# TensorE's loop from eight to nine rounds, two ring slots for the last V blocks, w_up in two parts and a one-matmul residual, in a decode kernel that streams a KV cache

## The chip, the cores and the metric

The kernel runs on one core of a Trainium2 chip. The metric is the device time of one execution in microseconds (us), the median of several executions. A profile is one further execution with the hardware profiler on; its span is 1.6 to 1.8 us shorter than the device time of that execution in the two main profiles. TensorE is the matrix engine, VectorE the vector engine, ScalarE the activation engine; GpSimd and SyncE are the other two. In the profile they are PE (PEld is its loading of weights), DVE, ACT, POOL and SP. SyncE issues nearly all transfers, on one queue (11560 of the 11568 packets in the page of the kernel before) that sixteen DMA engines serve together: the trace has sixteen reports for each transfer, and a transfer has landed with the last of them. The granted clock is the share of TensorE's full clock that the profile shows for a stretch of time. A run over 1.5% above the fastest of its kernel would count as slow.

## The reference, cut to what matters

```python
B, Sq, D = 1, 1, 512;  Hq, Hkv, Sk, Dh = 32, 8, 65536, 128;  F = 1792      # bfloat16
h  = x + A(layernorm(x))       # q = x@wq; softmax(q k^T / sqrt(Dh)) v; @wo
h2 = h + B(layernorm(h))       # (sigmoid(x@w_gate) * (x@w_up)) @ w_down
```

One token attends to a cache of 65536 positions and 8 KV heads. K and V are 134 MB each; with the weights 282.3 MB have to come from memory, each byte once.

## The kernel before: the parts that matter

K and V come in 32 blocks of 4 MB each (8 heads, 4 blocks per head). Of a K block, VectorE transposes eight pieces and TensorE multiplies them with the head's query; the softmax of a head follows after its fourth block; V products (`PV`) run one head behind. A ring of four 4 MB slots holds what has landed. The order of the loads, and who frees a slot:

```python
order = [("wq", 0)]
order += [("K", b) for b in range(NR)]
for b in range(NR, NB):
    order += [("K", b), ("V", b - NR)]
order += [("V", NB - 4), ("V", NB - 3), ("V", NB - 2), ("V", NB - 1), ("wg", 0), ("wu", 0), ("wd", 0)]
for i, ld in enumerate(order):
    slot_of[ld] = i % NSLOT
    prev[ld] = order[i - NSLOT] if i >= NSLOT else None
# a load waits for freed(prev): K by VectorE's transposes ("F"), V by its product ("PV")
# wo (4 MB, three transfers) is issued between V28 and V29
```

So a steady state has K in slots 1 and 3 and V in 0 and 2, but the last loads go round all four.

TensorE and VectorE run their instructions in a hardware loop. For TensorE a round `i` holds, for `r` in 0 to 3, part `A{r}` (scores of K block `4i+r`) and part `B{r}` (product of V block `4(i-1)+r`); the B parts are skipped in round 0:

```python
P.rounds = {"pe": (0, HKV), "dve": (1, HKV)}
...
with eng.Fori(lo, hi) as i:
    for p in order:
        with ExitStack() as cond:
            if lo not in parts[e][p]:
                cond.enter_context(eng.If_ne(i.val[eng.engine], lo))
            for o, w in zip(parts[e][p][hi - 1], plan[p]):
                put(e, eng, o, w)
```

What follows the eight rounds (the four V products of the last head, the wo product, the second block) is straight-line code. Its end, cut:

```python
# w_gate (gu0), the residual, then w_up (gu1)
for i, (nm, bank) in enumerate((("wg", GB), ("wu", UB))):
    for kt in range(4):
        for c in range(4):
            op("pe", ... matmul(ps(bank, ...), lhsT=hc[:, kt:kt + 1], rhs=wv[:, kt, c * FG:(c + 1) * FG]), ["hc", nm] ...)
    if i == 0:                      # residual h, 16 fp32 matmuls of 1x32 (32 passes)
        for g in range(4):
            for kt in range(4):
                op("pe", ... matmul(dst, lhsT=hT[1][:, kt:kt + 1], rhs=identf[:, 32 * g:32 * g + 32], start=(kt == 0) ...))
# sg = tanh (ScalarE), hh = product, hhT = transpose (VectorE)
for i, (r0, r1) in enumerate(WD_SPLIT):       # [(0, 7), (7, 12), (12, 14)]: w_down lands in three parts
    for r in range(r0, r1):
        for g in range(4):
            op("pe", ... matmul(ps(YB, 0, 128, ...), lhsT=hhT[:, 32 * r:32 * r + 1], rhs=wd_v[:, r, g * 128:(g + 1) * 128]), ["hhT", f"wd{i}"] ...)
# cast to bfloat16 (VectorE), output transfer
```

## Time and profile before

| quantity | value |
|---|---|
| device time | 664.56 us median of 3 runs (664.40 to 664.81) |
| profiled span | 662.6 us |
| TensorE / VectorE busy | 64% / 53% |
| bytes read | 282.33 MB, 426 GB/s over the span |
| last V block's first part released | 643.98 us |
| last matmul / output transfer issued | 659.93 / 660.30 us |

The first view is the page: busy time of the engines with its share of the span and the number of instructions, the DMA engines' busy share in 40 slices of 16.6 us (tenths, 9 means 90% or more), the bytes per second in each slice, and the queues with the share of the sixteen DMA engines' time. This is the kernel before.

```profile
PE 424.0 (64%) x2385; PEld 80.5 (12%) x1617; DVE 350.6 (53%) x443; ACT 38.1 (6%) x106; POOL 5.4 (1%) x12
DMA  9999999999999999999999999999999999999997
GB/s 380 439 420 435 437 423 437 433 423 441 429 425 441 425 431 439 423 436 433 425 437 433 425 439 431 425 437 431 427 439 425 433 435 425 437 433 410 426 427 292
q1 hardware_dynamic: 11560, 282.33, 99.3%
q8 instruction: 4, 0.07, 0.0%
q14 instruction: 2, 0.02, 0.0%
```

No slice but the last is below 90%, and the data queue's packets occupy 99.3% of all DMA engines' time. No compute engine is near that. Queues 8 and 14 carry a few packets of instructions.

The second view is the chain of waits, in order of time (start, us, what): from the middle of the span.

```profile
169.13 29.65 DMA ring<-in_A_k_cache_dram
198.81 9.13 DVE ktw L439 x8
207.98 29.65 DMA ring<-in_A_k_cache_dram
```

A K block is issued at 169.13, lands 29.65 us later, is transposed in 9.13 us, which frees its slot for the issue at 207.98. The period is 38.85 us, in which two K and two V blocks pass: 16.78 MB / 38.85 us = 432 GB/s. The 29.65 us from issue to landing are mostly time behind other blocks in the queue: at 432 GB/s the 4.19 MB of one block take 9.7 us (estimate).

The third view is the timeline of the end (start, us, engine, line, operation, in square brackets the idle time before and what ended it). `PS<-ring,PT_sb` are V products, `PS<-ring,hc` w_gate and w_up, `PS<-ring,hhT` w_down.

```profile
626.94 3.21 PE L529 MATMUL PS<-ring,PT_sb 128*16 128x512 bf16 x32 [3.32 <-DMA ring<-in_A_v_cache_dram]
...
643.98 3.22 PE L529 MATMUL PS<-ring,PT_sb 128*16 128x512 bf16 x32 [1.79 <-DMA ring<-in_A_v_cache_dram]
650.31 0.16 DVE L624 SCALAR_TENSOR_TENSOR hc<-PS,hT 128x4 bf16<-128x4 f32 x1 [0.50 <-PE PS L358]
652.27 1.20 PE L640 MATMUL PS<-identf,hT 128*1 128x32 f32 x32
655.17 0.93 PE L632 MATMUL PS<-ring,hc 128*1 128x448 bf16 x16 [1.70 <-DMA ring<-in_B_w_up_dram]
657.80 0.91 PE L656 MATMUL PS<-ring,hhT 128*1 128x128 bf16 x28 [1.70 <-DVE hhT L651]
658.91 1.02 PE L656 MATMUL PS<-ring,hhT 128*1 128x128 bf16 x28 [0.20 <-DMA ring<-in_B_w_down_dram]
659.98 0.29 DVE L660 CAST y_sb<-PS 128x128 bf16<-128x128 f32 x1 [2.24 <-PE PS L656]
```

The V products shown (V29, V31; V30 at 636.65 is left out), w_up's matmuls and the second part of w_down each start when their bytes land. The residual's 32 passes (652.27) run while TensorE waits for w_up.

### The profile page before, as it was taken

To read this page: it belongs to the slowest core of one execution; us is meant where nothing else is said; L and a number is where in the kernel's file an instruction comes from. 1 tells how busy PE (TensorE), PEld (TensorE's weight loads), DVE (VectorE), ACT (ScalarE), POOL (GpSimd) and SP (SyncE) were. 2 spreads that over 40 slices of the span, in tenths; PEclk is the share of its full clock that TensorE was granted. 3 is DMA by queue.
4 is the path that set the end of the run, shared out by engine and by line. 5 is a ranking of instruction groups with operands and counts; after the bars stand their busy time and mean duration, and the time that the engine had idled before them with its cause. 6 is when DMAs were issued, how large, how long until landed. Compare 5 with 4: busy or idle time off the path is not lost.

```text
span 662.6 us, 4910 instructions
## 1 busy us (share of the span) xinstructions
PE 424.0 (64%) x2385; PEld 80.5 (12%) x1617; DVE 350.6 (53%) x443; ACT 38.1 (6%) x106; POOL 5.4 (1%) x12
## 2 busy tenths in 40 slices
PE   2787487548676575576665576765856667556744
PEld 1100010011010110011100111001100111001222
DVE  3598855556337654347555463466643565553002
ACT  0200200020000200020000200002000200002000
POOL 2000000000000000000000000000000000000000
PEclk9799687678877677776866688766878867766877
DMA  9999999999999999999999999999999999999997
GB/s 380 439 420 435 437 423 437 433 423 441 429 425 441 425 431 439 423 436 433 425 437 433 425 439 431 425 437 431 427 439 425 433 435 425 437 433 410 426 427 292
DMA packets 11568, 282.42 MB, mean 426 GB/s; under 512 B 1193, under 2 KB 2218, under 8 KB 2602
## 3 DMA queue, kind: packets, MB, share of 16 engines
q1 hardware_dynamic: 11560, 282.33, 99.3%
q8 instruction: 4, 0.07, 0.0%
q14 instruction: 2, 0.02, 0.0%
q10 hardware_dynamic: 2, 0.00, 0.0%
HBM read 282.33 MB, written 0.00 MB: 426 GB/s over the span
## 4 chain that ended last, share of the span: by engine, by line
DMA 71%; DVE 22%; PE 6%; issue 1%; SPq 0%; ACT 0%
DMA ring<-in_A_k_cache_dram 62%; DVE ktw L439 20%; DMA ring<-in_A_v_cache_dram 4%; DMA ring<-in_B_w_down_dram 3%; PE PS L452 2%; DMA ring<-in_A_wq_dram 2%; PE PS L394 1%; PE PS L529 1%; DVE M_sb L444 1%; PE PS L451 1%; SPq L313 0%; DVE PT_sb L501 0%; PE PS L656 0%; PE PS L478 0%; PE PS L485 0%
## 5 line engine op out<-in xcount | busy, mean ns | idle before, releaser
L439 DVE STREAM_TRANSPOSE ktw<-ring 128x1024 f32<-128x1024 f32 x256 | 291.8, 1207 | 166.3 <-DMA ring<-in_A_k_cache_dram 165.3
L452 PE MATMUL PS<-ktw 128*128 128x512 bf16 x768 | 271.4, 452 | 54.2 <-DVE ktw L439 54.2
L451 PE MATMUL PS<-ktw 128*128 128x512 bf16 x256 | 119.0, 465 | 116.7 <-DVE ktw L439 114.9
L529 PE MATMUL PS<-ring,PT_sb 128*16 128x512 bf16 x1024 | 75.1, 444 | 12.8 <-DMA ring<-in_A_v_cache_dram 11.6
L451 PEld LDWEIGHTS PS<-ktw 128*128 128x128 bf16 x256 | 27.7, 108 | 432.8 <-issue 274.4
L501 DVE STREAM_TRANSPOSE PT_sb<-P_sb 128x512 bf16<-128x512 bf16 x32 | 20.2, 684 | 37.4 <-PE PS L539 36.0
L529 PEld LDWEIGHTS PS<-ring,PT_sb 128*16 128x16 bf16 x1024 | 30.6, 116 | 56.5 <-issue 30.0
L444 DVE TENSOR_REDUCE M_sb<-PS 128x1 f32<-128x512 f32 x32 | 19.9, 684 | 25.6 <-PE PS L451 25.6
L487 ACT ACTIVATE negmax<-PS 128x1 f32<-128x1 f32 x8 | 1.4, 171 | 545.8 <-PE PS L485 545.8
L491 ACT ACTIVATE P_sb<-PS,negmax 128x512 bf16<-128x512 f32 x32 | 21.5, 685 | 0.3
L508 DVE TENSOR_REDUCE lsum<-PS 128x1 f32<-128x4 f32 x8 | 1.3, 162 | 29.8 <-PE PS L506 29.8
L394 PE MATMUL PS<-ring,xz 128*8 128x512 bf16 x32 | 9.7, 478 | 7.4 <-DMA ring<-in_A_wq_dram 7.4
L354 DVE COPY hT<-PS 128x4 f32<-128x4 f32 x2 | 1.3, 629 | 24.9 <-PE PS L566 24.9
L478 PE MATMUL PS<-identf,gm 128*1 128x128 f32 x16 | 3.3, 292 | 17.0 <-DVE gm L476 17.0
L536 ACT ACTIVATE po_sb<-PS,rl 128x512 bf16<-128x512 f32 x8 | 5.7, 708 | 39.7 <-PE PS L529 39.7
L539 PE MATMUL PS<-sel_bf,po_sb 128*128 128x4 bf16 x32 | 2.1, 169 | 8.0 <-ACT po_sb L536 8.0
L485 PE MATMUL PS<-one_f,gmrep 1*128 1x1 f32 x16 | 4.0, 317 | 5.0 <-DVE gmrep L482 5.0
L491 ACT ACTIVATION_READ_ACCUMULATOR P_sb<-PS,negmax 128x1 f32 x32 | 6.5, 203 | 0.0
L369 POOL TENSOR_TENSOR rstd<-ve,nhalf 128x1 f32<-128x1 f32 x2 | 1.1, 553 | 645.7 <-DVE ve L367 645.7
L577 PE MATMUL PS<-ktw,O 128*1 128x512 bf16 x28 | 6.2, 379 | 0.0
L394 PEld LDWEIGHTS PS<-ring,xz 128*8 128x8 bf16 x32 | 3.2, 102 | 13.5 <-issue 11.3
L480 DVE TENSOR_REDUCE gmj<-PS 1x4 f32<-1x128 f32 x8 | 2.2, 278 | 4.1 <-PE PS L478 4.1
(85 smaller groups left out, 68.8 us busy)
## 6 DMA issues: line engine op xcount, KB each, us to landing
ring<-in_A_k_cache_dram SPq DMA_DIRECT2D x32, 4096.0 KB, 29.6
ring<-in_A_v_cache_dram SPq DMA_DIRECT2D x31, 4096.0 KB, 30.4
ring<-in_A_wq_dram SPq DMA_DIRECT2D x1, 4096.0 KB, 12.3
ring<-in_A_v_cache_dram SPq DMA_DIRECT2D x1, 3072.0 KB, 32.3
ktw<-in_A_wo_dram SPq DMA_DIRECT2D x1, 2048.0 KB, 9.6
ktw<-in_A_wo_dram SPq DMA_DIRECT2D x2, 1024.0 KB, 13.0
ring<-in_B_w_gate_dram SPq DMA_DIRECT2D x1, 1792.0 KB, 35.1
ring<-in_B_w_up_dram SPq DMA_DIRECT2D x1, 1792.0 KB, 24.9
```

Source lines behind the costliest of these rows:

```text
L394: op("pe", lambda e, kt=kt, n=n, last=last: e.matmul(ps(1, 0, 512, 0, 8), lhsT=xz[:, kt * 15 + 7 - n: kt * 15 + 15 - n], rhs=wq_v[:, kt, n ...
L439: op("dve", lambda e, d=dst, sr=src: e.transpose(d, sr), deps, f"T{b}.{c}", to="T")
L444: op("dve", lambda e, u=u: e.tensor_reduce(M_sb[:, u % 4:u % 4 + 1], ps(u % NS, 0, 512), AX.X, ALU.max), [f"S{b}.{NC - NR + k}"], f"mx{u}" ...
L451: return e.matmul(out, lhsT=lhsT, rhs=rhs, start=start, stop=stop)
L452: return e.add_instruction(mybir.InstMatmult(name=nc.get_next_instruction_name(), engine=mybir.EngineType.PE, ins=[e.lower_ap(rhs), e.lowe ...
L478: op("pe", lambda e: e.matmul(ps(MISC, 0, 128, 0, 1), lhsT=gm[:, :], rhs=identf[:, :], start=True, stop=True), [f"gm{h}"], f"gmT{h}", to="Q")
L485: op("pe", lambda e: e.matmul(ps(MISC, 128, 129), lhsT=gmrep[0:1, :], rhs=one_f[0:1, 0:1], start=True, stop=True), [f"gmrep{h}"], f"neg{h}")
L491: op("act", lambda e, b=b: e.activation(P_sb[:, (b % 4) * 512:(b % 4 + 1) * 512], ps(b % NS, 0, 512), AF.Exp, bias=negmax[:, k:k + 1], sca ...
L501: op("dve", lambda e, b=b: e.transpose(PT_sb[:, (b % 4) * 512:(b % 4 + 1) * 512], P_sb[:, (b % 4) * 512:(b % 4 + 1) * 512]), [f"E{b}", f"o ...
L529: op("pe", lambda e, lhsT=lhsT, tq=tq, t0=t0, c=c: e.matmul(ps(PO, 0, 512, 32 * tq, 32 * tq + 16), lhsT=lhsT, rhs=ring[:, s * SLOT + t0 * ...
L536: op("act", lambda e: e.activation(po_sb[:, :], ps(PO, 0, 512), AF.Copy, scale=rl[:, :]), [f"PV{NR * h + NR - 1}", f"rl{h}"], f"po{h}", to ...
L577: op("pe", lambda e, r=r, src=src, n=n, end=end: e.matmul(ps(YB, 0, D, 0, 1), lhsT=src[:, r:r + 1], rhs=ktw[:, r * D:(r + 1) * D], start=( ...
```

## The change

The intent: let the last head's four V products run in a ninth round of the same loop, instead of being written out again, so that TensorE's program gets shorter. The loop needs the same slot and the same waits for a V block in every round, so the last V blocks stay in slots 0 and 2. The K slots 1 and 3 are then free early and take w_gate, w_up and w_down. At the end, w_up is loaded in two parts so that three quarters of its product can run before the rest lands, and the residual becomes one fp32 matmul with a prepared operand `hz`. The diff, cut to its core (cuts marked with `...`):

```diff
-            order = [p for p, r in seq if r == hi - 1]
+            order = self.order[e]
...
-                        if lo not in parts[e][p]:
-                            cond.enter_context(eng.If_ne(i.val[eng.engine], lo))
-                        for o, w in zip(parts[e][p][hi - 1], plan[p]):
+                        if runs == [hi - 1]:
+                            cond.enter_context(eng.If_eq(reg, hi - 1))
+                        else:
+                            if runs[0] != lo:
+                                cond.enter_context(eng.If_ne(reg, lo))
+                            if runs[-1] != hi - 1:
+                                cond.enter_context(eng.If_lt(reg, runs[-1] + 1))
+                        for o, w in zip(parts[e][p][runs[-1]], plan[p]):
...
-            slot_of[ld] = i % NSLOT
-            prev[ld] = order[i - NSLOT] if i >= NSLOT else None
+            if ld[0] == "V" and ld[1] >= NB - NR:
+                slot_of[ld] = slot_of["V", ld[1] - 2]
+                prev[ld] = ("V", ld[1] - 2)
+            elif ld[0][0] == "w" and i:
+                slot_of[ld] = 3 if ld[0] == "wd" else 1
+                prev[ld] = ("K", NB - 1 if ld[0] == "wd" else NB - 2)
+            else: ...                                   # as before
...
+        W_SPLIT = {"wg": [(0, 4)], "wu": [(0, 3), (3, 4)]}
+        W_AT = {"wg": 0, "wu": 4 * FF}
...
-        P.rounds = {"pe": (0, HKV), "dve": (1, HKV)}
+        P.rounds = {"pe": (0, HKV + 1), "dve": (1, HKV)}
+        P.order = {"pe": ["A0", "B0", "L", "A1", "B1", "A2", "B2", "A3", "X", "C", "B3"], ...}
...                        # X: wait for the fourth V block, i = 1 to 7; C: only in the ninth round (i = 8)
...                        # L: wo product of heads 0-27, only in the ninth round
-            op("dve", lambda e: e.tensor_copy(yr[:, :], ps(YB, 0, D, 0, 1)), ["yr"], "yrs")
+            op("dve", lambda e: e.tensor_tensor(yr[:, :], ps(YB, 0, D, 0, 1), x_row[:, :], ALU.add), ["yr"], "yrs")
...
-                for g in range(4):
-                    for kt in range(4):
-                        ...                             # the residual's 16 fp32 matmuls
+                op("pe", lambda e: e.matmul(ps(YB, 0, 128), lhsT=gsel[:, :], rhs=hz[:, :], start=True, stop=False, ...), ["hz"])
```

Besides, one zeroing matmul and one matmul that added `x` are dropped; VectorE gets three small operations.

More of the change, by code (lines that the diff above doesn't have):

```diff
@@ L44, in __init__ @@
         self.rounds = {}
+        self.order = {}
         self.part = {}
@@ L147, in run @@
                 s2 = {}
-                w = [waits_of(e, o, s2, off, True) for o in parts[e][p][r]]
+                w = [waits_of(e, o, s2, off, len(parts[e][p]) > 1) for o in parts[e][p][r]]
                 assert plan.setdefault(p, w) == w, (p, r)
@@ L155, in run @@
                         off[k] = off.get(k, 0) + n
-            regs = {}
             with eng.Fori(lo, hi) as i:
                 for p in order:
+                    runs = sorted(parts[e][p])
+                    reg = i.val[eng.engine]
                     with ExitStack() as cond:
-                        if lo not in parts[e][p]:
-                            cond.enter_context(eng.If_ne(i.val[eng.engine], lo))
-                        for o, w in zip(parts[e][p][hi - 1], plan[p]):
+                        if runs == [hi - 1]:
+                            cond.enter_context(eng.If_eq(reg, hi - 1))
+                        else:
+                            assert runs == list(range(runs[0], runs[-1] + 1)) and runs[0] - lo < 2
+                            if runs[0] != lo:
[3 more added lines that the diff above has]
+                        for o, w in zip(parts[e][p][runs[-1]], plan[p]):
                             put(e, eng, o, w)
@@ L204, in bass_sequential_preLN__gqa_block_cached__glu_gated_glu__decode_kernel @@
         yr = sb("yr", [1, 512], fp32)
+        gsel = sb("gsel", [128, 128], fp32)
+        hz = sb("hz", [128, 128], fp32)
         scr = sb("scr", [1, 64], fp32)
@@ L275, in bass_sequential_preLN__gqa_block_cached__glu_gated_glu__decode_kernel @@
         for i, ld in enumerate(order):
-            slot_of[ld] = i % NSLOT
-            prev[ld] = order[i - NSLOT] if i >= NSLOT else None
+            if ld[0] == "V" and ld[1] >= NB - NR:
[4 more added lines that the diff above has]
+                prev[ld] = ("K", NB - 1 if ld[0] == "wd" else NB - 2)
+            else:
+                slot_of[ld] = i % NSLOT
+                prev[ld] = order[i - NSLOT] if i >= NSLOT else None
         def freed(ld):
@@ L296, in bass_sequential_preLN__gqa_block_cached__glu_gated_glu__decode_kernel @@
                 w = B_w_gate if k == "wg" else B_w_up
-                dma("sp", lambda e, d=dst, w=w: e.dma_start(d[:, 0:4 * FF].rearrange("p (k n) -> p k n", k=4),
-                    w.rearrange("(p k) n -> p k n", p=128)), f"r{s}", deps, k)
+                dst, src = dst[:, W_AT[k]:W_AT[k] + 4 * FF], w.rearrange("(p k) n -> p (k n)", p=128)
+                for i, (k0, k1) in enumerate(W_SPLIT[k]):
+                    dma("sp", lambda e, d=dst, w=src, a=k0 * FF, z=k1 * FF: e.dma_start(d[:, a:z], w[:, a:z]),
+                        f"{k}{i}", deps if i == 0 else (), f"{k}.{i}")
             elif k == "wd":
@@ L310, in bass_sequential_preLN__gqa_block_cached__glu_gated_glu__decode_kernel @@
                         dma("sp", lambda e, d=dst, sr=src, a=c0 * CH, z=c1 * CH: e.dma_start(d[:, a:z], sr[:, a:z]),
-                            f"vl{i}", deps if i == 0 else (), f"V{b}.{i}")
+                            "v0" if i else "vl", deps if i == 0 else (), f"V{b}.{i}")
                 else:
-                    dma("sp", lambda e, d=dst, sr=src: e.dma_start(d, sr), f"v{s}" if k == "V" and b < NB - NR else f"k{s}" if k == "K" and b >= NR else f"r{s}",
+                    dma("sp", lambda e, d=dst, sr=src: e.dma_start(d, sr), f"v{s}" if k == "V" else f"k{s}" if k == "K" and b >= NR else f"r{s}",
                         deps, f"{k}{b}")
@@ L348, in bass_sequential_preLN__gqa_block_cached__glu_gated_glu__decode_kernel @@
         op("dve", lambda e: e.tensor_copy(sel_bf[:, :], sel_f[:, :]), ["self"], "sel")
+        op("dve", lambda e: e.memset(gsel[:, :], 0.0), (), "gs0")
+        op("dve", lambda e: e.tensor_reduce(bass.AP(tensor=gsel, offset=0, ap=[[128, 128], [32, 4]]),
+                                            identf[:, :].rearrange("p (s j) -> p s j", s=4), AX.X, ALU.add), ["gs0", "identf"], "gsel")
         def ln_stats(i, src_dep, bank, c0):
@@ L378, in bass_sequential_preLN__gqa_block_cached__glu_gated_glu__decode_kernel @@
         op("pe", lambda e: e.matmul(ps(PO, 0, 512), lhsT=zrow[0:1, 0:128], rhs=zrow[0:1, :], start=True, stop=True),
-           ["zrow", "identf", "lsel", "onef", "sel"])
-        op("pe", lambda e: e.matmul(ps(5, 0, 128), lhsT=zrow[0:1, 0:128], rhs=zrow[0:1, 0:128], start=True, stop=True))
+           ["zrow", "identf", "lsel", "onef", "sel", "gsel"])
         ln_stats(0, ("xTp", (MISC, 0, 4)), 0, 0)
@@ L506, in denominators @@
             op("pe", lambda e: e.matmul(ps(MISC, 132, 136), lhsT=lsel[:, :], rhs=L_sb[:, :], start=True, stop=True),
-               [f"PT{NB - 1}"] if h == HKV - 1 else (), f"l{h}", to="Q")
+               [f"PT{NR * h + NR - 1}"], f"l{h}", to="Q")
             op("dve", lambda e: e.tensor_reduce(lsum[:, :], ps(MISC, 132, 136), AX.X, ALU.add), [f"l{h}"], f"ls{h}", to="D")
@@ L517, in pv @@
                     deps = []
-                    if b == NB - 1:
-                        for i, (c0, c1) in enumerate(V_SPLIT):
-                            if c == c0 and tq == 0:
-                                deps.append(f"V{b}.{i}")
-                    elif c == 0 and tq == 0:
-                        deps.append(f"V{b}")
+                    if tq == 0 and c == (V_SPLIT[1][0] if r == NR - 1 else 0):
+                        deps.append(f"V{b}" if b < NB - 1 else f"V{b}.1")
                     if c == 0 and tq == 0:
@@ L587, in columns @@
                                                               stop=False, skip_group_check=True), ["yrs"] if nt == 0 else ())
-            op("pe", lambda e: e.matmul(ps(YT, 0, 4), lhsT=ident[:, :], rhs=xT[:, :], start=False, stop=False,
-                                        skip_group_check=True), ["xT"], "yx")
-        P.rounds = {"pe": (0, HKV), "dve": (1, HKV)}
+        P.rounds = {"pe": (0, HKV + 1), "dve": (1, HKV)}
+        P.order = {"pe": ["A0", "B0", "L", "A1", "B1", "A2", "B2", "A3", "X", "C", "B3"],
+                   "dve": ["A0", "B0", "A1", "A2", "A3", "A4"]}
         P.loop_sems = {"T": ("pe", "A3", NR * NC), "g": ("pe", "A3", 2), "W": ("pe", "A3", 1), "PT": ("pe", "B3", 1),
@@ L596, in bass_sequential_preLN__gqa_block_cached__glu_gated_glu__decode_kernel @@
         for i in range(HKV + 1):
+            loop = 0 < i < HKV
             for r in range(NR):
-                b, v = NR * i + r, NR * (i - 1) + r
-                P.part = {"pe": (f"A{r}", i), "dve": (f"A{r}", i) if i else None} if i < HKV else {}
+                P.part = {"pe": (f"A{r}", i), "dve": (f"A{r}", i) if loop else None}
                 if i < HKV:
-                    dve_block(b)
-                    pe_scores(b)
+                    dve_block(NR * i + r)
+                    pe_scores(NR * i + r)
                     if r == NR - 1:
                         softmax(i)
-                P.part = {"pe": (f"B{r}", i), "dve": (f"B{r}", i)} if i < HKV else {}
                 if i:
+                    v = NR * (i - 1) + r
+                    if r == NR - 1 and i < HKV:
+                        P.part = {"pe": ("X", i)}
+                        op("pe", lambda e: None, [f"V{v}"])
+                    elif r == NR - 1:
+                        P.part = {"pe": ("C", i)}
+                        columns()
+                        op("pe", lambda e: None, [f"V{v}.0"])
+                    P.part = {"pe": (f"B{r}", i), "dve": (f"B{r}", i) if loop else None}
                     if r == 0:
@@ L612, in bass_sequential_preLN__gqa_block_cached__glu_gated_glu__decode_kernel @@
                     if v == NB - 4:
+                        P.part = {"pe": ("L", i)}
                         project7()
-                    if v == NB - 2:
-                        columns()
-            P.part = {"dve": ("A4", i) if i else None}
+            P.part = {"dve": ("A4", i) if loop else None}
             if i < HKV:
@@ L625, in bass_sequential_preLN__gqa_block_cached__glu_gated_glu__decode_kernel @@
                                                    op0=ALU.mult, op1=ALU.add), ["tot.1"], "hc")
+        op("dve", lambda e: e.tensor_tensor(hz[:, :].rearrange("p (j k) -> p j k", k=4),
+                                            bass.AP(tensor=sel_f, offset=0, ap=[[32, 128], [1, 32], [0, 4]]),
+                                            bass.AP(tensor=hT[1], offset=0, ap=[[4, 128], [0, 32], [1, 4]]), ALU.mult),
+           ["hT.1", "self"], "hz")
         ln_rstd(1, STB, 0, 4.0)
@@ L628, in bass_sequential_preLN__gqa_block_cached__glu_gated_glu__decode_kernel @@
         for i, (nm, bank) in enumerate((("wg", GB), ("wu", UB))):
-            wv = slot_ap(slot_of[(nm, 0)])[:, 0:4 * FF].rearrange("p (k n) -> p k n", k=4)
+            at = slot_of[(nm, 0)] * SLOT + W_AT[nm]
             for kt in range(4):
                 for c in range(4):
-                    op("pe", lambda e, wv=wv, kt=kt, c=c, bank=bank: e.matmul(
-                        ps(bank, 0, FG, 32 * c, 32 * c + 1), lhsT=hc[:, kt:kt + 1], rhs=wv[:, kt, c * FG:(c + 1) * FG],
+                    dep = [f"{nm}.{j}" for j, (k0, _) in enumerate(W_SPLIT[nm]) if k0 == kt and c == 0]
+                    op("pe", lambda e, at=at, kt=kt, c=c, bank=bank: e.matmul(
+                        ps(bank, 0, FG, 32 * c, 32 * c + 1), lhsT=hc[:, kt:kt + 1],
+                        rhs=ring[:, at + kt * FF + c * FG: at + kt * FF + (c + 1) * FG],
                         start=(kt == 0), stop=(kt == 3), tile_position=(0, 32 * c)),
-                       ["hc", nm] if kt == 0 and c == 0 else (), f"gu{i}" if kt == 3 and c == 3 else None)
+                       ["hc"] * (kt == 0 and c == 0) + dep, f"gu{i}" if kt == 3 and c == 3 else None)
             if i == 0:
-                for g in range(4):
-                    for kt in range(4):
-                        dst = psap(YB, kt, [[4, 32]], 32 * g, 1)
-                        op("pe", lambda e, g=g, kt=kt, dst=dst: e.matmul(
-                            dst, lhsT=hT[1][:, kt:kt + 1], rhs=identf[:, 32 * g:32 * g + 32],
-                            start=(kt == 0), stop=False, tile_position=(0, 32 * g), skip_group_check=True),
-                           ["hT.1"] if g == 0 and kt == 0 else ())
+                op("pe", lambda e: e.matmul(ps(YB, 0, 128), lhsT=gsel[:, :], rhs=hz[:, :], start=True, stop=False, skip_group_check=True),
+                   ["hz"])
         op("act", lambda e: e.activation(sg[:, :], ps(GB, 0, FG), AF.Tanh, scale=rstd[1][:, 0:1]), ["gu0", "rstd.1"], "sg")
```

## The prediction

> **What bounds the kernel now.** The DMA stream. The page shows it at 90% or more in every slice but the last, 426 GB/s over the span; TensorE is busy 64%, VectorE 53%. In the chain of waits two K and two V blocks (16.8 MB) come round every 38.86 us, which is 432 GB/s. In two-microsecond windows the stream never stops from 560 to 656 us. The timeline of the end shows stages released by their bytes: V29's product at 626.94, V30's at 636.65, V31's at 643.98, w_up's matmuls at 655.17. The last two parts of w_down release matmuls at 658.91 and about 659.54; then come a 0.29 us cast and the output DMA from 660.30. Only some 3 us of the 662.6 us span follow the last input byte.
>
> **What the change does, costed.**
> 1. Bytes: the same, 282.3 MB, in the same order on one queue. Splitting w_up adds 128 smaller packets, 8 per engine. In the trace a 14336-byte packet takes 539 ns, a 7168-byte one 274, a 5120-byte one 199[...], so roughly +0.1 us (estimate).
> 2. Slots: V29 now waits for PV27 (ends about 607.8) instead of PV26, V30 for PV28 (615.6), V31 for PV29 (630.2); the weights then wait for nothing. The queue gets shallower: at 615.6 V29 is still to land (626.9), at 630.2 V30 still has 6.4 us to run. It should not run dry. The weights' issue at 630 to 633 instead of 615.6, 630.2 and 640.2 buys nothing: they wait behind V31 anyway.
> 3. w_up in two parts: 12 of its 16 matmuls (0.93 us for all) go before the last quarter lands, so w_down's first matmuls start about 0.6 us before 657.80. But those 28 already ended about when w_down's second part came (wait 0.20 us). The gain becomes waiting there: 0 to 0.1 us.
> 4. Residual: 32 fp32 passes (1.20 us at 652.27) become one 128x128 fp32 product (about 0.3), with one VectorE product before it. They lie in a 1.70 us wait for w_up: gain 0. The dropped columns-matmul (0.18) and zero-matmul (0.31) lie in waits too; the two added VectorE setup operations lie before wq's landing at 13.
> 5. Loop: some seven more conditional parts per round[...] into TensorE waits of 3 to 6 us. [...] the page counts only six instruction packets for a kernel that already loops, so the loop stays resident. Round nine's skips fall in waits too. Gain and loss 0.
>
> **On the critical path:** practically nothing; sum -0.1 to +0.2 us.
>
> **Predicted time 664.5 us, 8 in 10 between 663.8 and 665.2.** Faster by over 2%: 0.01; within 2%: 0.98; slower: 0.01.
>
> **What would show it.** Step 1: GB/s per slice within 1% of before, last w_down landing within 0.5 us of 659.5. Step 2: V29 to V31 products at the same times, no DMA window below 300 GB/s between 604 and 656. Step 3: hhT ends about 0.6 us sooner, the wait for w_down's second part grows by as much. Step 4: the wait for w_up grows by about 0.9 us. Step 5: K period still 38.86 us.
>
> **What would make it wrong.** A queue that runs dry after 607 or 630 us (each dry microsecond costs one); a fetch stall over 3 us in round nine; packets shared unevenly among engines at the end.

The marked cuts, here and in the expectations below, took out what no run of this case shows. The forecast's sum came to -0.1 to +0.2 us, and it stands with terms cut: in step 1 a fixed time for each packet (the +0.1 us stays as the author's estimate from the three packet times), in step 5 the time of a branch and the cost of the loop a round, which had entered the sum as 0 because it was to fall in TensorE's waits (of 5.31, 3.76, 5.44 and 6.61 us, ended at 510.96, 533.43, 569.25 and 588.68 us, in the kernel before). The 0.3 us of step 4 is the author's estimate; the nearest thing in the kernel before, two fp32 matmuls with a 128x128 operand (L478), took 0.38 us at 524.17 and 0.58 at 602.29.

## The result, and the profile after

The changed kernel took 664.85 us (median of 4 runs, 664.48 to 665.43); the kernel before took 664.51 (4 runs, 664.40 to 664.81). Ratios in this document are the mean time of one kernel's fast runs over that of the other's of the same rounds, so not quite the ratio of the medians: here 1.0005, with a 95% interval from 0.9988 to 1.0022.

The page of the changed kernel (its DMA slices read 9 throughout, and 6 in the last):

```profile
PE 426.6 (64%) x2353; PEld 79.4 (12%) x1585; DVE 351.1 (53%) x446; ACT 38.7 (6%) x106; POOL 5.4 (1%) x12
GB/s 380 441 415 437 439 417 441 439 415 441 441 415 441 437 419 439 433 425 437 427 433 437 423 437 437 419 437 441 419 437 439 419 439 437 421 437 407 435 418 287
q1 hardware_dynamic: 11704, 282.33, 99.3%
q8 instruction: 3, 0.05, 0.0%
q14 instruction: 3, 0.02, 0.0%
```

The chain of waits of the changed kernel, in the middle of the span:

```profile
169.37 29.66 DMA ring<-in_A_k_cache_dram
199.05 9.13 DVE ktw L462 x8
208.23 29.64 DMA ring<-in_A_k_cache_dram
```

The timeline of its end:

```profile
627.22 3.36 PE L548 MATMUL PS<-ring,PT_sb 128*16 128x512 bf16 x32 [2.32 <-DMA ring<-in_A_v_cache_dram]
...
644.59 3.59 PE L548 MATMUL PS<-ring,PT_sb 128*16 128x512 bf16 x32 [2.07 <-DMA ring<-in_A_v_cache_dram]
651.55 0.16 DVE L649 SCALAR_TENSOR_TENSOR hc<-PS,hT 128x4 bf16<-128x4 f32 x1 [0.48 <-PE PS L382]
653.36 0.80 PE L668 MATMUL PS<-hz,gsel 128*128 128x128 f32 x2
654.28 1.66 PE L662 MATMUL PS<-ring,hc 128*1 128x448 bf16 x16
657.66 0.92 PE L682 MATMUL PS<-ring,hhT 128*1 128x128 bf16 x28 [1.73 <-DVE hhT L677]
659.12 1.02 PE L682 MATMUL PS<-ring,hhT 128*1 128x128 bf16 x28 [0.54 <-DMA ring<-in_B_w_down_dram]
660.19 0.29 DVE L686 CAST y_sb<-PS 128x128 bf16<-128x128 f32 x1 [2.61 <-PE PS L682]
```

The stream is the same: 99.3% again, period 38.86 us again, 426 GB/s again. In the middle of the span the changed kernel is already 0.24 us late (169.37 against 169.13), before any of the end's changes acts; w_down's second part comes 0.21 us later (659.12 against 658.91), and so do the cast and the end. So most of the 0.3 us between the two profiled spans was there from the first rounds on.

Inside the end, something did change. The vector `hc`, from which w_gate and w_up are multiplied, was begun 1.24 us later (651.55 against 650.31), and the wait for w_up, 1.70 us before, was gone. Still the products with hhT began 0.14 us sooner, and waited 0.54 us instead of 0.20 for w_down. That calls for a test: either these shifts are all absorbed by the stream, or a loss (the loop) and a gain (the split, the residual) cancel.

### The profile page after: what moved, and what is told of

It is laid out like the page before. It is cut to its first block, busy times and chain, and to the rows that moved or that the text cites. A ratio compares the mean times of both kernels' runs of the same rounds, so it can differ in the third digit from the quotient of the medians.

```text
span 662.9 us, 4929 instructions
## 1 busy us (share of the span) xinstructions
PE 426.6 (64%) x2353; PEld 79.4 (12%) x1585; DVE 351.1 (53%) x446; ACT 38.7 (6%) x106; POOL 5.4 (1%) x12
## 3 DMA queue, kind: packets, MB, share of 16 engines
q1 hardware_dynamic: 11704, 282.33, 99.3%
## 4 chain that ended last, share of the span: by engine, by line
DMA 66%; DVE 22%; PE 9%; issue 1%; SPq 0%; ACT 0%; DVEq 0%
DMA ring<-in_A_k_cache_dram 58%; DVE ktw L462 20%; PE PS L475 4%; DMA ring<-in_B_w_down_dram 4%; DMA ring<-in_A_v_cache_dram 3%; DMA ring<-in_A_wq_dram 2%; PE PS L548 2%; PE PS L474 1%; PE PS L417 1%; DVE M_sb L467 1%; DVE PT_sb L524 1%; PE PS L508 0%; SPq L318 0%; PE PS L501 0%; PE PS L682 0%
## 5 line engine op out<-in xcount | busy, mean ns | idle before, releaser
L548 PE MATMUL PS<-ring,PT_sb 128*16 128x512 bf16 x1024 | 79.1, 462 | 16.4 <-DMA ring<-in_A_v_cache_dram 10.8
L508 PEld LDWEIGHTS PS<-one_f,gmrep 1*128 1x128 f32 x16 | 3.7, 286 | 7.7 <-DVE gmrep L505 7.7
```

Of the source, the lines that this page charges most:

```text
L508: op("pe", lambda e: e.matmul(ps(MISC, 128, 129), lhsT=gmrep[0:1, :], rhs=one_f[0:1, 0:1], start=True, stop=True), [f"gmrep{h}"], f"neg{h}")
L548: op("pe", lambda e, lhsT=lhsT, tq=tq, t0=t0, c=c: e.matmul(ps(PO, 0, 512, 32 * tq, 32 * tq + 16), lhsT=lhsT, rhs=ring[:, s * SLOT + t0 * ...
```

## The experiments

Theory A: the byte stream sets the end, and each part of the change only moves waiting. Theory B: the loop costs about a microsecond and the split with the residual pays it back. A third reading, theory L, came out of the DMA packets of the trace and is introduced at its experiments. Eleven kernels ran. They ran in four batches on different chips; each ratio is to the kernel before in the same batch, whose median was 664.39 to 664.67.

| kernel | median us (runs) | ratio to before | 95% interval |
|---|---|---|---|
| changed, w_up in one part | 664.89 (5) | 1.0003 | 0.9990 to 1.0017 |
| loop and slots only | 664.33 (5) | 0.9998 | 0.9985 to 1.0012 |
| split and residual only | 664.73 (5) | 1.0006 | 0.9993 to 1.0020 |
| slots only | 664.44 (5) | 1.0005 | 0.9992 to 1.0019 |
| changed, half of V's bytes | 537.76 (2) | 0.8092 | 0.8076 to 0.8108 |
| changed, 24 more conditionals a round | 664.84 (4) | 1.0008 | 0.9991 to 1.0024 |
| changed, 512 GpSimd memsets in a line | 665.43 (5) | 1.0024 | 1.0010 to 1.0037 |
| changed, 1024 in a line | 668.13 (5) | 1.0055 | 1.0041 to 1.0069 |
| changed, 2048 in a line | 673.24 (4) | 1.0131 | 1.0114 to 1.0148 |
| changed, 2048 in a loop | 664.83 (4) | 1.0004 | 0.9988 to 1.0021 |
| changed, TensorE's small products cut | 664.58 (5) | 1.0004 | 0.9990 to 1.0017 |

### 1. Each part alone

**Loop and slots only.**

```diff
 # against the changed kernel
-        W_SPLIT = {"wg": [(0, 4)], "wu": [(0, 3), (3, 4)]}
+        W_SPLIT = {"wg": [(0, 4)], "wu": [(0, 4)]}
-                op("pe", ... matmul(ps(YB, 0, 128), lhsT=gsel[:, :], rhs=hz[:, :], ...))       # and hz
+                ...                       # the 16 fp32 matmuls and the zeroing matmul of before
```

> The changed kernel without the w_up split and with the residual added by 32 small passes again: the loop and the slots alone. Theory A: ratio to before between 0.999 and 1.0015, last part of w_down lands within 0.5 us of before's. Theory B: TensorE's tail is about 1.3 us late (as hc was in the changed kernel, 651.55 against 650.31) and nothing pays it back, so 665.3 to 666 us; a quarter to a half of a microsecond at the end would be between the two, since the slack before w_down's second part was 0.20 us.

It took 664.33 us, the lowest median of all. The end of its timeline:

```profile
651.62 0.16 DVE L650 SCALAR_TENSOR_TENSOR hc<-PS,hT 128x4 bf16<-128x4 f32 x1 [0.68 <-PE PS L382]
658.13 0.56 PE L684 MATMUL PS<-ring,hhT 128*1 128x128 bf16 x28 [1.70 <-DVE hhT L679]
658.90 0.45 PE L684 MATMUL PS<-ring,hhT 128*1 128x128 bf16 x20 [0.20 <-DMA ring<-in_B_w_down_dram]
659.96 0.29 DVE L688 CAST y_sb<-PS 128x128 bf16<-128x128 f32 x1 [1.88 <-PE PS L684]
```

TensorE's tail was as late as in the changed kernel (hc at 651.62), nothing pays it back, and w_down's second part and the cast come when they did before (658.90 and 659.96 against 658.91 and 659.98). Theory B, which wanted 665.3 to 666, falls. (Not all of that lateness is the loop's: point 4 of the last part takes it apart.)

**Split and residual only.** The kernel before, with the changed kernel's `W_SPLIT`, `gsel`, `hz` and the one residual matmul, and the old slots and loop.

> The kernel before with the w_up split and the one-matmul residual, nothing else. Theory A: within 0.3 us of before; the products with hhT start 0.4 to 0.7 us before 657.80 and wait that much longer for w_down's second part. Theory B: 0.5 to 1 us faster than before, about 663.7.

664.73 us: no gain. The two lines of its timeline that decide:

```profile
657.65 0.92 PE L663 MATMUL PS<-ring,hhT 128*1 128x128 bf16 x28 [1.71 <-DVE hhT L658]
659.11 1.02 PE L663 MATMUL PS<-ring,hhT 128*1 128x128 bf16 x28 [0.55 <-DMA ring<-in_B_w_down_dram]
```

The products with hhT started 0.15 us earlier than before, not 0.4 to 0.7: a size was missed, the same as in the prediction (below). The wait for w_down grew from 0.20 to 0.55. The gain became waiting. The split and the residual were tested together here; no run has the one-matmul residual alone.

**Slots only.** The kernel before, with the changed kernel's `slot_of` and `prev`, and w_gate and w_up in one slot.

> The kernel before with the new slots alone (last V blocks in two slots, w_gate and w_up in one, so V30 and V31 are issued about 4 to 6 us before the stream would run dry). Theory A: within 0.3 us of before, no two-microsecond DMA window below 300 GB/s from 604 to 656, V products at the same times as before to 0.3 us. Rival: the shallower queue costs stream time, V31 lands 0.5 us or more later.

664.44 us. V29 to V31's products started at 627.45, 637.16 and 644.48 in its profile, about 0.5 us later than before, against the 0.3 foreseen; but its K blocks were already 0.46 us late in the middle (169.59 against 169.13), so the lateness does not come from the slots. The lowest two-microsecond DMA window from 604 us to 656 us was 344 GB/s, as in the kernel before. The shallower queue costs nothing that can be seen. In this profile the 56 products with hhT ran without a wait for w_down, from 658.90, and the cast began at 660.62; the next run shows the same.

**The changed kernel with w_up in one part.**

```diff
-        W_SPLIT = {"wg": [(0, 4)], "wu": [(0, 3), (3, 4)]}
+        W_SPLIT = {"wg": [(0, 4)], "wu": [(0, 4)]}
```

> The changed kernel with w_up loaded in one part again. Theory A (the byte stream sets the end, the parts of the change only move waits): total within 0.4 us of the changed kernel; the products with hhT start about 0.3 to 0.8 us later than the changed kernel's 657.66, and the wait for the second part of w_down (0.54 us) shrinks to about 0 to 0.2. Theory B (the loop costs time and the split pays it back): the whole delay arrives at the end, total 0.5 us or more above the changed kernel.

The median of 664.89 us agrees with theory A. The expectation for its profile missed: the profiled run was the slowest of its five (666.34 us; the other four lay between 664.55 and 665.08). In it, w_up released its matmuls only at 657.13, 1.6 to 2 us later than in the profiles of the other kernels without the split (655.16 to 655.54), and the 56 products with hhT then ran without any wait. One DMA engine was late there; section 4 shows how that comes about.

```profile
657.13 1.66 PE L662 MATMUL PS<-ring,hc 128*1 128x448 bf16 x16 [2.51 <-DMA ring<-in_B_w_up_dram]
660.49 1.66 PE L682 MATMUL PS<-ring,hhT 128*1 128x128 bf16 x56 [1.70 <-DVE hhT L677]
```

Here theory A needs an exception. In eleven of the thirteen profiles the cast begins 0.47 to 0.48 us after w_down's last bytes land. In this one it is 0.77 us (662.20 after 661.43), and with slots only 0.79 (660.62 after 659.83). These two have w_up in one part and a granted clock of 0.50 from 656 to 660 us: w_up's 16 matmuls took 1.66 us, against 0.93 in the kernel before, and TensorE, not the bytes, came last. So the split saves some 0.3 us in such executions. The medians do not resolve it (664.89 without the split, 664.85 with it).

### 2. What is the stream worth, and how close is the compute behind it?

```diff
+                    if k == "V":
+                        dst, src = dst[:, 0:SLOT // 2], src[:, 0:SLOT // 2]
```

> The changed kernel with only the first half of V blocks 0 to 30 loaded (wrong result on purpose): 65.0 MB less of 282.3, same instructions on every compute engine. Theory A: the time falls by up to 65.0 MB / 432 GB/s = 150 us, to 514 us, unless TensorE (427 us busy) with its hand-overs becomes the limit first, so between 514 and 545 us. Rival (the compute chain is nearly as long as the stream): 600 us or more.

The products then use stale data in the upper halves. (The comparison with the reference passed nevertheless, so its tolerance doesn't see this; the run is used for its time alone.) It took 537.76 us, 127.1 us less than the changed kernel's 664.85, with the same instructions on every engine. The page:

```profile
PE 385.2 (72%) x2353; PEld 77.4 (14%) x1585; DVE 350.1 (65%) x446; ACT 38.7 (7%) x106; POOL 5.4 (1%) x12
q1 hardware_dynamic: 11704, 217.32, 95.9%
```

65.0 MB fewer at 432 GB/s would be 150 us. The stream is now busy 95.9% instead of 99.3%, so compute has begun to show: from its chain of waits, K's period for a whole head is about 59.7 us (94.98 to 453.42 for six heads), where the bytes alone, 25.2 MB / 432 GB/s, need 58.2. The kernel with all its bytes takes 77.7 us a head, so compute would fit with some 18 us a head to spare. A part of that has to come off: with half of V's bytes TensorE was granted more clock (0.849 on the mean, against 0.765) and was busy 385.2 us against 426.6, which is 5 us a head. Some 13 us a head is left (estimate).

### 3. What do the conditional parts cost?

```diff
                 for p in order:
+                    if e == "pe" and p == "X":
+                        for _ in range(24):
+                            with eng.If_lt(i.val[eng.engine], 99):
+                                pass
```

> The changed kernel with 24 more empty conditional parts in each of the nine rounds, in front of the wait before each fourth V product. [...] Theory A: no change of the total beyond 0.3 us (the stream is 6 us or more ahead)[...]. Rival (conditional parts cost time as they are executed)[...].

664.84 us, no change. By the 2.97 us a round measured below, the rival would have added 27 us over nine rounds (estimate). The line of V27's product, first of the kernel before, then of the changed kernel, then of this one:

```profile
604.17 3.61 PE L529 MATMUL PS<-ring,PT_sb 128*16 128x512 bf16 x32
```

```profile
605.44 3.61 PE L548 MATMUL PS<-ring,PT_sb 128*16 128x512 bf16 x32 [0.79 <-issue]
```

```profile
608.37 3.61 PE L552 MATMUL PS<-ring,PT_sb 128*16 128x512 bf16 x32 [3.76 <-issue]
```

The change made TensorE wait 0.79 us for its own sequencer where before it waited for nothing. Twenty-four more conditionals add 2.97 us, so one that is entered costs 0.124 us. The author's estimate had counted two branches for each. The trace has one: 340 compare-and-branch records on TensorE against 124 in the changed kernel, which is 216 more, one for each of 24 in nine rounds, and from one to the next it is 123 ns. A part that is skipped costs more: in the changed kernel it is mostly 0.26 to 0.32 us from its branch to the next one. The cost is real, and it is paid in every round, and it does not reach the end.

### 4. Where the tenths of a microsecond come from: instruction fetches on the DMA engines

The last question was why profiles of nearly equal kernels differ by some tenths of a microsecond from their first rounds on, and one by 2 us at its end. The trace has each DMA packet with its start, duration and size, but not its engine; which packets share an engine is inferred from ends and starts that meet. A 32 KB data packet takes 1.218 us on its DMA engine. Listing the instruction packets and the slowed data packet that starts when each of them ends gives this (kernel before; times in us on the packets' own clock, which runs 10.95 us ahead of the span):

```
instruction packet           the data packet after it
 47.523  1.045  16384 B       48.552  1.694  32768 B
 65.695  0.325   8192 B       66.008  1.875  32768 B
 67.944  1.016  16384 B       68.945  1.764  32768 B
308.541  0.312   8192 B      308.850  1.595  32768 B
634.256  1.026  16384 B      635.267  1.764  32768 B
660.866  1.079  16384 B      661.930  1.027  14336 B   (0.539 else)
```

The 16 KB packets are those of queue 8, taken for TensorE's because it loses one when TensorE's program is cut (below); the 8 KB packets are those of queue 14. Read this way, an instruction fetch occupies one DMA engine for its own duration, and the data packet after it takes 0.35 to 0.66 us longer (the least of these with GpSimd's fetches below): about 1.5 us for a 16 KB fetch (1.05 + 0.46), 0.66 to 0.98 us for an 8 KB one. Theory L says that this lag stays to the end: each transfer is cut evenly over the sixteen engines, every engine always has work queued, so the engine that lost 1.5 us never makes it up, and a landing counts only when the latest engine is done. The packets agree: chained by end and start, with 4 ns between them, those of the kernel before make sixteen chains, each with 511 to 513 of the 8192 packets of 32 KB.

The trace can be asked directly. Each transfer raises its semaphore sixteen times, read here as one report for each engine. In the kernel before, the latest report comes 0.11 us after the second latest for the block that lands at 32.46 us. TensorE's first fetch starts at 36.57, and for the next block, at 43.38, it comes 1.20 us after. From there to V31's first part, at 643.93, the latest report stays 1.5 to 1.6 us behind the median one, where it was 0.36 for the block at 32.46: the lag is kept. For the block that lands near 170 us, the latest report lies behind the median one by 1.53 us in the kernel before and by 1.80 in the changed kernel. This difference of 0.27 us accounts for the 0.24 by which the changed kernel was late in the middle of the span.

The test adds fetches from the idle GpSimd.

```diff
         ln_rstd(0, 0, 0, 1.0)
+        for j in range(2048):
+            op("pool", lambda e, j=j: e.memset(pscr[:, j:j + 1], 0))
```

> The changed kernel with 2048 one-byte memsets on the otherwise idle GpSimd, in a straight line: 128 KB of instructions to fetch. Theory L (an instruction fetch delays the one DMA engine that carries it, and that engine stays late to the end, because its ring is always full and every transfer is cut evenly over 16 engines): the traces show jumps of 0.4 to 1.5 us in one engine's lag per 16 KB fetch, so 8 fetches on one engine mean the last landing and the total 4 to 10 us later. Rival (128 KB is 0.3 us of a shared stream): under 0.5 us later.

and as a control the same memsets in a loop of 32 times 64:

> Control: the same number of memsets on GpSimd, in a loop of 32 times 64, so nearly nothing more to fetch. Theory L: total within 0.4 us of the changed kernel. If the memsets themselves disturb[...], this is as slow as the straight-line form.

The straight-line form took 673.24 us, the loop 664.83. GpSimd's timeline in the straight-line form:

```profile
31.57 4.27 POOL L409 MEMSET pscr<- 1x1 uint8 x128 [1.23 <-issue]
```

After every 128 memsets GpSimd stalls 1.2 us, and queue 14 carries an 8 KB packet every 5.5 us until the memsets end: 18 packets instead of the control's 3 (the page's line; packets, MB and share):

```profile
q14 instruction: 18, 0.15, 0.1%
```

The 15 packets more, 123 KB, are 0.3 us of a 432 GB/s stream; they cost 8.4. The chains of waits show when. First the straight-line form, then the loop:

```profile
178.01 29.65 DMA ring<-in_A_k_cache_dram
255.72 29.65 DMA ring<-in_A_k_cache_dram
```

```profile
169.60 29.65 DMA ring<-in_A_k_cache_dram
247.37 29.61 DMA ring<-in_A_k_cache_dram
```

At 178 us, some 80 us after the last of the added fetches, the stream is 8.41 us behind the control, and at 255.72 it is 8.35 behind: the lag was made early and kept, while the period stayed 38.85 us. That a single engine holds the lag is seen in the sixteen reports (below), and where the issue of V29 and V30 has to wait for products of blocks that land late. Stretches of 4 us (the last three columns: granted TensorE clock, mean busy share of the 16 DMA engines, GB/s); first the straight-line form, then the loop:

```profile
606.00:610.00 4.00, 2.53 (x12) 0.19 (x2) 2.08 (x4) 0.00 (x0) 0.00 (x0) 1.00 0.06 25
```

```profile
606.00:610.00 4.00, 2.04 (x24) 0.54 (x12) 1.10 (x2) 1.68 (x6) 0.00 (x0) 0.50 0.96 410
```

A mean share of 0.06 is one engine of sixteen. The sixteen reports agree: for the block that landed at 615.56 us fifteen had come by 607.00, so the latest was 8.56 us behind, against 8.68 for the block at 178.52. Fifteen engines had run out of work, and one was still working off what the fetches had put before it.

**The dose.** The same with 512 and 1024 memsets.

> As the straight-line form with 2048 memsets (673.24 us, 8.4 us over the looped control, 16 more fetches of 8 KB), but 512 memsets, 4 more fetches. If every fetch adds the same 0.53 us to the engine that is latest anyway: about 2.1 us over the control, near 666.9. If GpSimd's fetches fall on another DMA engine than the one that TensorE's fetches have already made 1 to 2 us late, they hide behind it at first: 0 to 0.6 us over the control.

> 1024 memsets in a straight line, 8 more fetches of 8 KB. Same engine: about 4.2 us over the control, near 669.0. Another engine, hidden at first: 2 to 3 us over the control. If the fetches were spread over all engines: under 0.4 us.

The sixteen reports for the block that lands near 170 us in the control, and the times:

| GpSimd memsets | fetches by GpSimd | latest report after the median, us | after the second latest, us | landing, us | device time, us |
|---|---|---|---|---|---|
| 2048 in a loop | 1 | 1.95 | 0.53 | 170.11 | 664.83 |
| 512 in a line | 4 | 2.50 | 0.85 | 170.64 | 665.43 |
| 1024 in a line | 8 | 4.96 | 3.51 | 173.19 | 668.13 |
| 2048 in a line | 16 | 10.47 | 8.68 | 178.52 | 673.24 |

Over the looped control (664.83) the three doses cost 0.60, 3.30 and 8.41 us for 4, 8 and 16 fetches by GpSimd (counted in the packets; the control has one of them). The smallest dose is uncertain: two of its five runs took 666.7 and 666.8 us, and by the means it costs 1.06. It and the middle one ran on another chip than the control. From 4 to 8 fetches it is 0.68 us each, from 8 to 16 it is 0.64, and the packets say 0.66 (0.31 of fetch, 0.35 of slower data packet). Each dose is 2.0 to 2.2 us short of 0.66 a fetch (2.6, 5.3 and 10.6): the first 2 us are hidden. So the engine that GpSimd's fetches hit would without them be about 2 us ahead of the latest one. The reports show this: in the control the latest engine is 1.95 us behind the median. They also show that TensorE's fetches make other engines late. With 512 memsets the latest report is 2.36 us behind the second at 34.67 us, before TensorE's first fetch; at 54.10, after its second, the two next engines have come up to 0.87 and 1.00 us, and the latest itself is where it was (2.52 and 2.50 us behind the median). The expectation for the hidden case read 0 to 0.6 and 2 to 3; the larger dose came a little above, because it was worked out with 0.53 us a fetch, from the first test, where the hidden part had diluted it.

**The opposite direction: fewer fetches.** TensorE's program was cut.

```diff
+                if kt and not last:                   # wq: 9 matmuls of 32
+                    continue
+                    if not deps and not last:         # each V product: 2 or 3 of 32
+                        continue
-            regroup(0)                                # wo of heads 0-27: 4 rows of 28
-            regroup(1)
-            for r in range(r0, r1):                   # w_down parts 1 and 2: one row each
+            for r in range(r1 - 1 if i < 2 else r0, r1):
```

> The changed kernel with most of TensorE's small products left out (wrong result on purpose): of 32 matmuls of each V product 2 or 3 stay, of the wo product of heads 0 to 27 four rows, of wq's 32 nine, of w_down's first two parts one row each. All 282.3 MB are still loaded in the same order. TensorE loses about 75 us of busy time[...]. Theory A alone: no change, 664.6 to 665. Theory A with theory L: TensorE's three fetches of 16 KB (1.5 us each on the engine that carries them) disappear, the latest engine is then one with an 8 KB fetch (0.7 to 1 us), so the last landing comes 0.5 to 1.2 us earlier and the time is 663.4 to 664.2. Rival (TensorE's work sets part of the time): 5 us or more faster.

The result was wrong (relative error 0.82), and the time 664.58 us. TensorE lost 64 us of busy time and the time did not move, which is theory A again. The hoped-for microsecond did not come, and this test of theory L was not clean: its page still shows queue 8 with two packets of 16 KB,

```profile
PE 362.7 (55%) x1288; PEld 47.7 (7%) x520; DVE 350.3 (53%) x442; ACT 37.0 (6%) x106; POOL 5.4 (1%) x12
q8 instruction: 2, 0.03, 0.0%
```

one of them after the stream had ended, the other at 57.6 us on the packets' clock, in front of nearly the whole stream. One 16 KB fetch is enough to make one engine late: the latest report is 0.01 us behind the second for the block at 41.99 us, and 1.48 us for the next, at 53.18, after the fetch at 46.3 us of the span. Whether a program with none ends a microsecond sooner stays open.

The disturbed profile of the kernel with w_up in one part fits the same picture: in the packets of that run the latest engine ended 1.3 us behind the next one, and TensorE's last 16 KB fetch, at 665.7 on the packets' clock, fell into the transfer of w_up that came late. The sixteen reports show the step: the latest is 0.12 us behind the second for the transfer that landed at 651.48, and 1.31 us for w_up at 657.08, after that fetch at 654.5 us of the span. So the fetch hit one of the engines that were already latest. Single runs of other kernels also lie 1 to 2 us above their median (666.45 with slots only, 665.78 of the kernel before); they were not profiled, and whether they have the same cause is not shown.

No experiment points to a version that beats both kernels: all those with the full program and without the added memsets lie within 0.6 us of each other.

## Why the prediction was right, point by point

The time (664.85 in a range from 663.8 to 665.2) and the mechanism held: the byte stream sets the end, and what the change does to TensorE ends in waits, but for the 0.3 us of the split told in section 1. Experiment 1 shows it for the slots alone and for two pairs of parts, experiment 2 shows the stream as the limit by removing bytes. In detail:

1. Bytes. Right: 99.3% and 426 GB/s as before, and TensorE's last matmuls were released at 659.76 against 659.54. The test as worded ("GB/s per slice within 1%") failed: single slices differ by up to 3.7% (437 against 421 GB/s in the 35th), so slices of 16.6 us are too short for such a test. Over the span nothing differs. Of w_up's packets the trace has 10752 and 3584 bytes in 406 and 140 ns, where one of 14336 took 540: the split costs each engine 8 times 6 ns, less than the 0.1 us allowed.
2. Slots. Right: no two-microsecond window between 604 and 656 us fell under 320 GB/s, and slots alone changed nothing. Products started 0.3, 0.3 and 0.6 us later; 0.24 of this was there already at 169 us.
3. w_up in two parts. Mechanism right, size wrong. The step "w_down's first matmuls start about 0.6 us before 657.80" measured 0.14 (and 0.15 with the split alone). The prediction took the 0.93 us that w_up's 16 matmuls had needed at the full clock and gave three quarters of it back. In the changed profile TensorE ran at half clock in this stretch (granted 0.50 from 654 to 656 us, against 1.00), so the four matmuls left after the landing took about 0.55 us, from 655.39 to 655.94; and the landing itself was 0.22 later. That the gain becomes waiting for w_down was right: 0.20 to 0.54 us. What the step left out is the half clock without the split, when there is no waiting left (section 1).
4. Residual. The gain of 0 was right; "the wait for w_up grows by about 0.9 us" was wrong: it vanished. The step that failed is the unstated one that hc would come at the same time. It came 1.24 us later: 0.61 because V31's product started later (0.27 because its bytes landed later, 644.21 against 643.93, and 0.34 because two branches of the loop stand between the landing and the first matmul), 0.38 because it ran slower (3.59 against 3.22 us, at a granted clock of 0.58 against 0.67 between 644 and 648 us), and 0.30 at the end of the loop, from ScalarE's read of that product to the wo product (1.57 against 1.27 us; 1.57 also in the kernel with loop and slots only, 1.29 with split and residual only); 0.05 was won back behind it. The residual itself took 0.80 us, not the estimated 0.3, at half clock (granted 0.50 from 652 to 654 us).
5. Loop. Right that it costs the total nothing, but "round nine's skips fall in waits too" was wrong for V31. In the changed kernel's trace two compare-and-branch instructions follow its landing (at 644.23 and 644.46), and the product starts 0.39 us after the landing. It is 0.38 to 0.39 in all ten profiles with the ninth round, and 0.04 in the three without it (before, slots only, split and residual only). With the 0.30 us at the end of the loop this is 0.64 us on TensorE's path to hc, which the waits for w_up and w_down took up. Right, too, that nothing is fetched again in later rounds: TensorE's fetches stand at 36, 46 and 655 us of the span and nowhere between. The fetch stall that the prediction named among the risks did not come; no run here shows one on TensorE. The loop's cost on the sequencer is one compare-and-branch for each part: 0.124 us where it is entered (24 in a row, experiment 3) and mostly 0.26 to 0.32 where it is skipped.

What the prediction did not see is how instruction fetches set the last tenths. It named "packets shared unevenly among engines at the end" as a risk, without a cause; theory L gives one.

## What to carry to other kernels

When one stream is busy over 99%, as it was here (99.3%), cost a change by whether it alters the stream's bytes, its gaps, or what follows its last byte; everything else only moves waiting, and shifts of a microsecond in a tail that waits twice more for data should be expected to vanish, as long as those waits are longer than the shift. Here hc came 1.24 us later and the cast 0.21. Before trusting a tenth of a microsecond in such a tail, check the granted clock in that stretch: w_up's sixteen matmuls took 0.93 us in one profile and 1.66 in another. And keep straight-line instruction streams short on every engine, even an idle one, since their fetches take their turn on the same DMA engines, and the latest engine sets every landing: 16 fetches of 8 KB for 2048 memsets on GpSimd cost 8.41 us over the same memsets in a loop, with one fetch.
